# Attention scores in two bursts per unit, and products that wait for half of their operand

## The chip, the cores and the metric

The kernel runs on one core of one Trainium2 chip. The time is device microseconds of a whole execution, the median of several runs. The core has TensorE (matrix products, PE in the profile), VectorE (DVE), ScalarE (ACT), GpSimd (POOL) and SyncE (SP, which here only issues transfers), each with its own queue of instructions. Matrix products land in PSUM, which has eight banks here; only VectorE and ScalarE empty them in this kernel.

## The reference

Two layers, one behind the other. Attention without softmax, for 8 batches, 12 heads, 448 positions and 64 elements a head:

```python
scores = scale * np.matmul(q, k.transpose(0, 1, 3, 2))
attn = np.maximum(scores, 0.0) ** 2 / S
x = np.matmul(attn, v)                  # heads side by side: 3584 x 768
h = x @ w_in                            # 768 x 2048
g = np.maximum(h, 0.0) ** 2
out = g @ w_out                         # 2048 x 768
```

## The kernel before

**Units and rounds.** A batch is cut into three units of four heads, 24 units (`NUN`) in all. A unit's scores are made in seven rounds (`TJ`), one for every 64 keys, so the whole kernel has 168 rounds. A round is four matmuls of 64x64 weights and 448 columns (L522), which run at once on the four quarters of the array, and fills two PSUM banks. `squared` (L534) empties each bank with max(.,0) on VectorE (L538) or ScalarE (L541) into a `rel` tile, and squares that on ScalarE (L545) or GpSimd (L548) into an `at` tile, of which there are 11. When all seven rounds of a unit are squared, its AV (`av`, L568) multiplies them with v: 28 matmuls, again in quarters, into two banks, which VectorE or ScalarE copies to `xt` (L608, L610).

**Dense work.** When a batch's three AVs are done, `push_dense` (L946) queues its dense work. The first layer has 16 groups (`h_group`, L657), one for each block of 128 of the 2048 rows of g: six full-array matmuls of 448 columns (L650), then ScalarE squares the bank (L639) and VectorE masks by sign (L634) into the block of g. The second layer takes two chunks of 128 tokens together (`o_groups`, L833) and uses seven products in place of eight, as Strassen's method does: m1, m2, m6, m5, m7, m3, m4, each of eight matmuls of 384 columns (L863). They multiply a half of g (eight blocks), or a sum of halves (s1 to s4, VectorE, L842), with a part of w_out or a combination of parts; parts are gathered by copies (L783, L785) and by multiply-adds (L875), and go to memory.

**What a product waits for.** `evac_g` enters each masked block of g in `g_ops[b]`. `chunk` (L770) hands all of that list to `o_groups` as `ready`, so each product and each sum that reads g waits for all 16 blocks of its batch.

**The order of the work.** The kernel has manual scheduling. The program first lists operations (`plan.add`, `plan.pe`) with costs, dependencies, buffers and due times; then `Plan.simulate` plays the engines forward and writes down the order in which each engine gets its instructions. TensorE takes what is ready and due soonest. An operation can be glued to the one ahead of it (`glue`, L182): TensorE then takes that one next if it is ready, waits up to 0.45 us in the plan for it if it will be ready by then, and takes other work if not. The plan charges a switch between quarter mode and full mode at L50. `run` (L75) tries 16 rules, and with each up to six fits of the landing times of transfers, and keeps the plan that ends first among those whose landing times agree.

**The main loop** (L1100) goes over pairs of rounds. Each pair is entered as one burst, then a share of the queued dense work (`run_some`). The AV of unit n is glued behind the pair at index (7(n+1)-1)//2+2, four or five rounds after the unit's last round, and with `MERGE` the next pair is glued behind the AV, so that burst has four rounds and an AV. The first 21 rounds, the start-up and the first batch's first layer are written out before the loop.

Of the kernel before, what the change touches and what calls it, by code (L numbers as in the profile page):

```python
# [42 lines left out]
class Plan:  # L43
# [31 lines left out]
    def run(self):  # L75

        for z, op in enumerate(self.ops):
            op.id = z
        for op in reversed(self.ops):
            if not op.fixed or op.alts[0][0] != "PE":  # L80
                took = min(a[2] for a in op.alts)
                if len(op.alts[0]) > 4 and op.alts[0][4]:
                    took = 7.0
                due = min([x.due for x in op.nexts] or [1e6]) - took - 0.1
                op.due = due if op.due is None else min(op.due, due)
        start = {name: list(slots) for name, slots in self.pools.items()}, dict(self.busy)
        uses = [(b, b.left) for b in {b for op in self.ops for b in op.bufs}]

        def once(landing, rules):
            self.landing, (self.patience, self.lead) = dict(landing), rules  # L90
            self.pools = {name: list(slots) for name, slots in start[0].items()}
            self.busy, self.sent, self.order = dict(start[1]), [], []
            for b, left in uses:
                b.left, b.end, b.tile = left, 0.0, None
            self.simulate()
            return max(op.end for op in self.ops)

        best = None
        for rules in ((p, q) for p in self.PATIENCE for q in self.LEAD):
            landing: dict = {}  # L100
            for _ in range(6):
                try:
                    end = once(landing, rules)
                except RuntimeError:
                    break
                self.land()
                late = max(t - landing.get(z, 0.0) for z, t in self.landing.items())
                if late < 0.4 and (best is None or end < best[0]):
                    best = end, landing, rules
                landing = self.landing  # L110
        once(*best[1:])
        alone = None
        for emit, op in self.order:
            got = emit()
            if op is None:
                continue
            if len(op.way) > 5:
                alone = got
            elif alone is not None and op.engine == "POOL" and not op.size:
                self.behind(got, alone)  # L120
                alone = None
        return best[0]
# [175 lines left out]
def kernel(  # L298
# [11 lines left out]
    B, H, S, D = q.shape  # L310
# [5 lines left out]
    P = 128  # L316
    TP = 64
    TJ = S // TP
    NU = 3
    NUN = B * NU  # L320
# [303 lines left out]
    def evac_g(op, bank, b, fs, cols):  # L624
        g = gts[b]
        w = cols.stop - cols.start

        def views():
            src = bank.tile[:, 0:len(fs) * w].rearrange("p (f c) -> p f c", c=w)
            return src, g.tile[:, fs[0]:fs[-1] + 1, cols]  # L630

        def mask():
            src, dst = views()
            nc.vector.scalar_tensor_tensor(  # L634
                out=dst, in0=src, scalar=0.0, in1=dst, op0=ALU.is_gt, op1=ALU.mult)

        def sq():
            src, dst = views()
            nc.scalar.activation(out=dst, in_=src, func=AF.Square)  # L639

        one = plan.add([act(len(fs) * w, sq)], [op], [bank, g], due=plan.now + 0.3)
        two = plan.add([dve(len(fs) * w, mask)], [one], [bank, g], due=plan.now + 0.9)
        g_ops.setdefault(b, []).append(two)

    def h_mms(bank, b, f, cols, c0):
        w = cols.stop - cols.start
# [40 lines left out]
    def h_first():  # L687

        work = []
        for two in range(2):  # L690
# [28 lines left out]
            def turn(two=two, buf=buf, marks=marks):  # L719
# [8 lines left out]
                def copy(fn):  # L728
# [2 lines left out]
                        ps.tile.bitcast(FP16).rearrange("p (f c) -> p f c", c=P))  # L731

                op = plan.pe(0.057 * NH, flip, list(marks), [ps, buf])
                g_ops.setdefault(0, []).append(plan.add(
                    [("DVE", 0.62, 0.7, copy(nc.vector.tensor_copy)),
                     ("ACT", 0.93, 1.02, copy(nc.scalar.copy))], [op], [ps, g],
                    due=plan.now + 0.3))

            work += [(0.2157 * NM, wide(z, 2 * two + z)) for z in range(2)]
            work.append((0.057 * NH, turn))  # L740
# [14 lines left out]
    LO, HI = slice(0, HALF), slice(HALF, DM)  # L755
    rests: dict = {}

    def rest(pr):
        buf = Buf("rest")
        ops = []  # L760
        for i in range(2):
            b = 2 * pr + i

            def emit(i=i, b=b):
                return nc.gpsimd.tensor_copy(buf.tile[:, :, 64 * i:64 * i + 64],  # L765
                                             gts[b].tile[:, :, 3 * P:S])
            ops.append(plan.add([("POOL", 1.55, 1.6, emit)], g_ops[b], [buf, gts[b]]))
        rests[pr] = ops, buf

    def chunk(b, c):  # L770
        return (lambda: g_ops[b], lambda: gts[b], lambda: gts[b].tile[:, :, c * P:(c + 1) * P],
                [(b, 2 * c), (b, 2 * c + 1)])

    def rest_chunk(pr):
        return (lambda: rests[pr][0], lambda: rests[pr][1], lambda: rests[pr][1].tile,
                [(2 * pr, TJ - 1), (2 * pr + 1, TJ - 1)])

    def copied(op, bank, part):
# [54 lines left out]
    def o_groups(one, two):  # L833
# [11 lines left out]
        def sums():  # L845
            vec = nc.vector
            combine("s1", vec.tensor_add, ready2(), [buf2()],
                    lambda: view2()[:, lo], lambda: view2()[:, hi])
            combine("s2", vec.tensor_sub, ready1() + [st["s1"][0]], [buf1(), st["s1"][1]],
                    lambda: st["s1"][1].tile, lambda: view1()[:, lo])  # L850
            combine("s3", vec.tensor_sub, ready1() + ready2(), [buf1(), buf2()],
                    lambda: view1()[:, lo], lambda: view2()[:, lo])
            combine("s4", vec.tensor_sub, ready1() + [st["s2"][0]], [buf1(), st["s2"][1]],
                    lambda: view1()[:, hi], lambda: st["s2"][1].tile)

        def product(bank, lhs, deps, srcs, w, first, last=True):
# [28 lines left out]

        def m1():
            sums()
            op = product("x", lambda: view1()[:, lo], ready1() + [w2_ops[0][0]], [buf1()],
                         w2[0][0], True)
            part("r1", "x", op)  # L890

        def m2():
            op = product("y", lambda: view1()[:, hi], ready1() + [w2_ops[0][1]], [buf1()],
                         w2[0][1], True)
            close(at1, LO, "y", op, "r1")

# [19 lines left out]
            close(at1, HI, "z", op, "r2")  # L916

        def m4():
            op = product("w", lambda: view2()[:, hi], ready2() + t_ops["t4"], [buf2()], t4, True)
            close(at2, LO, "w", op, "r3", -1.0)  # L920

        return [(0.1625 * NH, fn) for fn in (m1, m2, m6, m5, m7, m3, m4)]
# [64 lines left out]
    EARLY = 6  # L987
    PLAIN0 = False
    NPE = 6
    MERGE = True  # L990
    ROUNDS = NUN * TJ
    NB = ROUNDS // 2
    STREAM = NU * TJ

    def av_burst(n):
        return (TJ * (n + 1) - 1) // 2 + 2

    pushes = {av_burst(NU * b + 2): b for b in range(1, B)}
    avs = {av_burst(n): n for n in range(NU, NUN)}

    idle = pools["part"][0].bitcast(FP16)[:, 0:512]
    nc.vector.memset(idle, 0.0)
# [91 lines left out]
    push_dense(0)  # L1094

    def coming(n):
        return plan.now + 4.5 * (TJ * n - 2 * i) / 2

    skipped, chain = 0, None
    for i in range(STREAM // 2, NB):  # L1100
        rs = [divmod(r, TJ) for r in range(max(STREAM, 2 * i), 2 * i + 2)]
        for n in range(NU, NUN):
            if i == max(STREAM // 2, TJ * (n - 2) // 2 + 1):
                if n >= EARLY:
                    for w in "kq":
                        raws[n, w] = load_qk(n, w, max(50.0, coming(n) - 20.0), n < EARLY + 2)
                if n not in vst:
                    load_v(n, coming(n) - 6.0)
            if i == max(STREAM // 2, (TJ * (n - 1) + 1) // 2 - 2) and n > 3:
                if n >= EARLY:  # L1110
                    for w in "kq":
                        casts[n, w] = cast_qk(n, w, raws[n, w])
# [3 lines left out]
                else:  # L1116
                    for w in "kq":
                        turn_dma(n, w, casts[n, w])
        todo = []
        for n, t in rs:  # L1120
            sp = [Buf("mm"), Buf("mm")]
            op = scores([(n, t)], sp, WHOLE, False)
            todo.append((op, sp, n, t))
            if chain is not None:
                chain.glue = op
            chain = op
        for op, sp, n, t in todo:
            second, at = square(op, sp, S)
            ats[n, t] = second, at, lambda tl: tl
        if i in avs:  # L1130
            last, chain = chain, av(avs[i], list(range(TJ)))
            last.glue = chain
        if i in pushes:
            push_dense(pushes[i])
        if i in avs and MERGE and i + 1 < NB:
            skipped = 1
            continue
        nxt = min([j for j in pushes if j > i] or [NB + 2])
        run_some(max(0.0, (queued - 4.0) * (1 + skipped) / (nxt - i + skipped)))
        skipped, chain = 0, None  # L1140
    run_some(3.0)
    for j in sorted(j for j in avs if j >= NB):
        av(avs[j], list(range(TJ)))
    for j in sorted(j for j in pushes if j >= NB):
        push_dense(pushes[j])
    ending = True
    run_some(1e9)
    plan.run()
# [30 lines left out]
```

## Time and profile before

The median of three runs is 381.44 us (380.92 to 383.48); the profiled execution spans 380.1 us.

| | busy us | share of the span | instructions |
|---|---|---|---|
| TensorE matmuls | 369.7 | 97% | 3277 |
| VectorE | 274.9 | 72% | 468 |
| ScalarE | 272.8 | 72% | 592 |
| GpSimd | 220.7 | 58% | 270 |

Busy time of TensorE counts from an instruction's start to its modelled end, and successive matmuls overlap; so rates are better read from the starts of rows than from their durations. In a row of the timeline the columns are start and duration in us, engine, line, operation, result and operands, shape and count; a bracket at the end is idle time of the engine ahead of the row and what ended it. The chain of work that ended last is followed back from the last instruction, at each step to what released it or to the instruction before it on its engine.

### The profile page before, as it was taken

How to read it: one execution, taken by the hardware profiler on the slowest of the kernel's cores; microseconds unless marked ns; L12 is line 12 of the kernel's file. 1: busy time of each engine (PE TensorE's matmuls, PEld its weight loads, DVE VectorE, ACT ScalarE, POOL GpSimd, SP SyncE). 2: the span in 40 equal slices, each digit the busy share in tenths (PEclk: the TensorE clock that was granted, in tenths of full speed). 3: DMA queues.
4: the chain of work that ended last, by engine and by line, in shares of the span. 5: the costliest groups of instructions: out<-in, count | busy, mean ns of one | idle time of the engine just before them, and what ended most of it. 6: DMA issues, size and time to landing. Idle time of an engine off the chain costs nothing.

```text
span 380.1 us, 8791 instructions
## 1 busy us (share of the span) xinstructions
PE 369.7 (97%) x3277; PEld 195.5 (51%) x3277; DVE 274.9 (72%) x468; ACT 272.8 (72%) x592; POOL 220.7 (58%) x270
## 2 busy tenths in 40 slices
PE   7899999999999999999999999999999999999995
PEld 3545655444455445444554555545555545555563
DVE  2996899977987787577997576676796668256731
ACT  4998999787956897697887675886795785244221
POOL 7999886596877786486663856574781343000100
PEclk9999999999999999999999999999999999999999
DMA  9999998699759943878347864685443002210243
GB/s 182 185 207 203 204 230 239 143 200 136 180 154 214 221 113 75 174 211 134 81 111 184 209 164 75 187 173 137 88 94 95 3 0 60 62 26 0 64 104 83
DMA packets 70218, 51.36 MB, mean 135 GB/s; under 512 B 36896, under 2 KB 70176, under 8 KB 70176
## 3 DMA queue, kind: packets, MB, share of 16 engines
q1 hardware_dynamic: 52384, 35.86, 38.8%
q0 software_dynamic: 16928, 14.09, 25.3%
q10 hardware_dynamic: 864, 0.85, 0.7%
q8 instruction: 25, 0.41, 0.4%
q14 instruction: 17, 0.14, 0.1%
HBM read 45.61 MB, written 11.01 MB: 149 GB/s over the span
## 4 chain that ended last, share of the span: by engine, by line
PE 89%; POOL 3%; DVE 3%; DMA 2%; ACT 1%; issue 1%; POOLq 0%; DVEq 0%
PE mm L650 38%; PE mm L863 32%; PE mm L522 9%; PE mm L588 8%; DMA g<-in_k_dram 2%; DVE comb L842 1%; DVE rel L538 1%; POOL w L496 1%; POOL comb L548 1%; PE mm L460 1%; PE mm L699 1%; POOL vs L489 1%; ACT at L545 1%; POOL g L406 0%; ACT g L729 0%
## 5 line engine op out<-in xcount | busy, mean ns | idle before, releaser
L548 POOL TENSOR_TENSOR at<-rel 128x448 f16<-128x448 f32 (+1 forms) x147 | 132.8, 924 | 62.7 <-DVE rel L538 43.9
L650 PE MATMUL mm<-xt,w 128*128 128x448 f16 (+1 forms) x768 | 148.7, 346 | 0.0
L634 DVE SCALAR_TENSOR_TENSOR g<-mm,g 128x448 f16<-128x448 f32 (+1 forms) x128 | 77.2, 605 | 45.3 <-ACT g L639 45.1
L538 DVE TENSOR_SCALAR rel<-mm 128x448 f32<-128x448 f32 (+3 forms) x174 | 96.8, 595 | 18.0 <-PE mm L522 16.8
L650 PEld LDWEIGHTS <-w 128*128 128x128 f16 x768 | 72.2, 98 | 71.1 <-issue 12.4
L639 ACT ACTIVATE g<-mm 128x448 f16<-128x448 f32 (+1 forms) x128 | 68.9, 540 | 46.3 <-PE mm L650 44.8
L545 ACT ACTIVATE at<-rel 128x448 f16<-128x448 f32 (+1 forms) x189 | 100.3, 586 | 0.8 <-PE mm L588 0.5
L541 ACT ACTIVATE rel<-mm 128x448 f32<-128x448 f32 (+2 forms) x174 | 84.6, 547 | 6.1 <-PE mm L522 5.8
L863 PEld LDWEIGHTS <-comb 128*128 128x128 f16 x448 | 42.4, 98 | 33.9 <-issue 5.2
L440 POOL CAST blk<-raw 128x896 f16<-128x896 f32 x36 | 33.9, 953 | 33.0 <-issue 7.7
L522 PE MATMUL mm<-qkt,qkt 64*64 64x448 f16 (+2 forms) x756 | 51.3, 337 | 0.8 <-DVE rel L538 0.4
L783 ACT ACTIVATE part<-mm 128x384 f32<-128x384 f32 x46 | 22.7, 500 | 39.7 <-PE mm L863 39.6
L875 DVE SCALAR_TENSOR_TENSOR part<-mm,part 128x384 f32<-128x384 f32 x56 | 30.4, 552 | 18.9 <-ACT part L783 11.5
L863 PE MATMUL mm<-wt,comb 128*128 128x384 f16 x224 | 39.5, 326 | 0.6 <-DVE comb L842 0.6
L863 PE MATMUL mm<-w,comb 128*128 128x384 f16 x224 | 39.6, 327 | 0.3 <-DVE part L785 0.3
L863 PEld LDWEIGHTS <-g 128*128 128x128 f16 x288 | 27.6, 98 | 20.7 <-issue 2.8
L588 PE MATMUL mm<-at,vs 64*64 64x448 f16 (+1 forms) x672 | 35.2, 343 | 0.2
L863 PE MATMUL mm<-w,g 128*128 128x384 f16 x192 | 33.7, 326 | 0.0
L489 POOL DMA_DIRECT2D vs<-in_v_dram x48 | 30.0, 632 | 2.6 <-DMA g<-in_k_dram 1.9
L522 PEld LDWEIGHTS <-qkt 64*64 64x64 f16 x756 | 17.7, 105 | 25.3 <-issue 21.1
L588 PEld LDWEIGHTS <-vs 64*64 64x64 f16 x756 | 21.8, 107 | 14.3 <-issue 3.2
L765 POOL COPY rest<-g 128x1024 f16<-128x1024 f16 x8 | 8.8, 1096 | 32.7 <-DVE comb L842 32.4
(59 smaller groups left out, 201.5 us busy)
## 6 DMA issues: line engine op xcount, KB each, us to landing
out_dram<-part SPq DMA_DIRECT2D x108, 96.0 KB, 2.2
raw<-in_k_dram SPq DMA_DIRECT2D x18, 448.0 KB, 4.0
raw<-in_q_dram SPq DMA_DIRECT2D x18, 448.0 KB, 4.8
vs<-in_v_dram POOLq DMA_DIRECT2D x48, 112.0 KB, 4.6
w<-in_moe_w_in_dram POOLq DMA_DIRECT2D x4, 768.0 KB, 12.0
w<-in_moe_w_out_dram POOLq DMA_DIRECT2D x4, 768.0 KB, 13.5
g<-in_k_dram POOLq DMA_DIRECT2D x4, 224.0 KB, 11.2
g<-in_q_dram POOLq DMA_DIRECT2D x4, 224.0 KB, 10.3
```

Source lines behind the costliest of these rows:

```text
L440: return lambda: fn(blk.tile.rearrange("p t (f d) -> p f t d", f=2), tile_of().rearrange("p f (t d) -> p f t d", d=D))
L489: return lambda: nc.gpsimd.dma_start(out=buf.tile[64 * r:64 * r + 64], in_=src[:, u, hs])
L522: nc.tensor.matmul(sp[e].tile[64 * c:64 * c + 64, c0:c0 + w].rearrange("p (t c) -> p t c", c=TP), lhsT=kT[r, t, 64 * e:64 * e + 64], rhs=q ...
L538: dve(width, lambda: nc.vector.tensor_scalar(out=r.tile[:, 0:width], in0=bank.tile[:, 0:width], scalar1=0.0, scalar2=SK, op0=ALU.max, op1= ...
L541: act(width, lambda: nc.scalar.activation(out=r.tile[:, 0:width], in_=bank.tile[:, 0:width], func=AF.Relu, scale=SK))],
L545: act(width, lambda: nc.scalar.activation(out=dst(), in_=r.tile[:, 0:width], func=AF.Square)),
L548: lambda: nc.gpsimd.tensor_mul(dst(), r.tile[:, 0:width], r.tile[:, 0:width]))],
L588: nc.tensor.matmul(banks[f].tile[64 * e:64 * e + 64, c0:c0 + w], lhsT=vs[r, e ^ c, t * D:(t + 1) * D], rhs=a[r, e, :], start=(t == 0), sto ...
L634: nc.vector.scalar_tensor_tensor(out=dst, in0=src, scalar=0.0, in1=dst, op0=ALU.is_gt, op1=ALU.mult)
L639: nc.scalar.activation(out=dst, in_=src, func=AF.Square)
L650: nc.tensor.matmul(bank.tile[:, c0:c0 + w], lhsT=w1[f // 4][:, m, f % 4 * P:(f % 4 + 1) * P], rhs=xts[b].tile[:, m, cols], start=(m == 0), ...
L863: nc.tensor.matmul(buf.tile[:, 0:HALF], lhsT=lhs()[:, j, :], rhs=w[:, j, :], start=(first and j == 0), stop=(j == NH - 1), skip_group_chec ...
```

## The change

Four things change.

1. The loop over pairs gives way to a list of bursts. Up to round 41 it repeats the old bursts. From unit 6 on (the third batch) each unit has two: four rounds, with the AV of the unit before glued in between the second and the third, and then three rounds. The dense work is shared out by rounds. The aim is fewer changes between small matmuls and dense ones.
2. `g_ops` keeps for each block which half of g and which columns it fills, and `filled` picks those that a reader needs: the products and sums that read one half of g wait for that half alone.
3. The plan tries up to ten fits of the landing times for each rule, and from the fifth on a landing time only moves later.
4. Loads and transposes of q and k are entered when the first round of a burst has reached their mark.

The diff, cut to its core:

```diff
-            for _ in range(6):
+            for turn in range(10):
...
+                if turn > 3:
+                    for z, t in self.landing.items():
+                        self.landing[z] = max(t, landing.get(z, 0.0))
...
-        g_ops.setdefault(b, []).append(two)
+        g_ops.setdefault(b, []).append((two, fs[0] // NH, cols))
...
+    def filled(b, half, cols):
+        return [op for op, h, c in g_ops[b]
+                if half in (None, h) and c.start < cols.stop and cols.start < c.stop]
...
-            combine("s2", vec.tensor_sub, ready1() + [st["s1"][0]], [buf1(), st["s1"][1]],
+            combine("s2", vec.tensor_sub, ready1(0) + [st["s1"][0]], [buf1(), st["s1"][1]],
...
-            combine("s3", vec.tensor_sub, ready1() + ready2(), [buf1(), buf2()],
+            combine("s3", vec.tensor_sub, ready1(0) + ready2(0), [buf1(), buf2()],
...
-            combine("s4", vec.tensor_sub, ready1() + [st["s2"][0]], [buf1(), st["s2"][1]],
+            combine("s4", vec.tensor_sub, ready1(1) + [st["s2"][0]], [buf1(), st["s2"][1]],
...
-            op = product("x", lambda: view1()[:, lo], ready1() + [w2_ops[0][0]], [buf1()],
+            op = product("x", lambda: view1()[:, lo], ready1(0) + [w2_ops[0][0]], [buf1()],
...
-            op = product("y", lambda: view1()[:, hi], ready1() + [w2_ops[0][1]], [buf1()],
+            op = product("y", lambda: view1()[:, hi], ready1(1) + [w2_ops[0][1]], [buf1()],
...
-            op = product("w", lambda: view2()[:, hi], ready2() + t_ops["t4"], [buf2()], t4, True)
+            op = product("w", lambda: view2()[:, hi], ready2(1) + t_ops["t4"], [buf2()], t4, True)
...
+    FIRST = (((21,), None), ((22, 23), None), ((24, 25), None), ((26, 27), None), ((28, 29), None),
+             (range(30, 34), 3), ((34, 35), None), ((36, 37), None), (range(38, 42), 4))
+    STEPS = (0, 1, 2, 3), (4, 5, 6)
...
+    def bursts():
+        for rs, n in FIRST:
+            yield list(rs), n
+        for n in range(2 * NU, NUN):
+            r = TJ * n
+            for step in STEPS:
+                yield [r + z for z in step], (n - 1 if step[0] == 0 else None)
+        yield [], NUN - 1
...
-    for i in range(STREAM // 2, NB):
+    for steps, done in bursts():
...
+        for z, r in enumerate(steps):
+            if z == 2 and done is not None:
+                chain = link(av(done, list(range(TJ))))
+            n, t = divmod(r, TJ)
+            sp = [Buf("mm"), Buf("mm")]
+            chain = op = link(scores([(n, t)], sp, WHOLE, False))
+            second, at = square(op, sp, S)
...
+            run_some(max(0.0, (queued - 4.0) * len(steps) / (nxt + 3 - now)))
```

More of the change, by code (lines that the diff above doesn't have):

```diff
@@ L733, in turn @@
                 op = plan.pe(0.057 * NH, flip, list(marks), [ps, buf])
-                g_ops.setdefault(0, []).append(plan.add(
+                done = plan.add(
                     [("DVE", 0.62, 0.7, copy(nc.vector.tensor_copy)),
                      ("ACT", 0.93, 1.02, copy(nc.scalar.copy))], [op], [ps, g],
-                    due=plan.now + 0.3))
+                    due=plan.now + 0.3)
+                g_ops.setdefault(0, []).append((done, two, PARTS[0]))
             work += [(0.2157 * NM, wide(z, 2 * two + z)) for z in range(2)]
@@ L766, in emit @@
                                              gts[b].tile[:, :, 3 * P:S])
-            ops.append(plan.add([("POOL", 1.55, 1.6, emit)], g_ops[b], [buf, gts[b]]))
+            ops.append(plan.add([("POOL", 1.55, 1.6, emit)], filled(b, None, slice(3 * P, S)), [buf, gts[b]]))
         rests[pr] = ops, buf
     def chunk(b, c):
-        return (lambda: g_ops[b], lambda: gts[b], lambda: gts[b].tile[:, :, c * P:(c + 1) * P],
+        cols = slice(c * P, (c + 1) * P)
+        return (lambda half=None: filled(b, half, cols), lambda: gts[b], lambda: gts[b].tile[:, :, cols],
                 [(b, 2 * c), (b, 2 * c + 1)])
     def rest_chunk(pr):
-        return (lambda: rests[pr][0], lambda: rests[pr][1], lambda: rests[pr][1].tile,
+        return (lambda half=None: rests[pr][0], lambda: rests[pr][1], lambda: rests[pr][1].tile,
                 [(2 * pr, TJ - 1), (2 * pr + 1, TJ - 1)])
@@ L989 @@
     NPE = 6
-    MERGE = True
+    FIRST = (((21,), None), ((22, 23), None), ((24, 25), None), ((26, 27), None), ((28, 29), None),
+             (range(30, 34), 3), ((34, 35), None), ((36, 37), None), (range(38, 42), 4))
+    STEPS = (0, 1, 2, 3), (4, 5, 6)
     ROUNDS = NUN * TJ
-    NB = ROUNDS // 2
     STREAM = NU * TJ
[L995 to L999, printed above, removed]
+    def bursts():
[6 more added lines that the diff above has]
+        yield [], NUN - 1
     idle = pools["part"][0].bitcast(FP16)[:, 0:512]
@@ L1096, in coming, with reached @@
     def coming(n):
-        return plan.now + 4.5 * (TJ * n - 2 * i) / 2
-    skipped, chain = 0, None
-    for i in range(STREAM // 2, NB):
-        rs = [divmod(r, TJ) for r in range(max(STREAM, 2 * i), 2 * i + 2)]
+        return plan.now + 2.25 * (TJ * n - now)
+    seen: set = set()
+    def reached(what, n, at):
+        if now < at or (what, n) in seen:
+            return False
+        seen.add((what, n))
+        return True
+    for steps, done in bursts():
+        now = steps[0] if steps else ROUNDS
         for n in range(NU, NUN):
-            if i == max(STREAM // 2, TJ * (n - 2) // 2 + 1):
+            if reached("load", n, TJ * (n - 2) + 2):
                 if n >= EARLY:
@@ L1108 @@
                     load_v(n, coming(n) - 6.0)
-            if i == max(STREAM // 2, (TJ * (n - 1) + 1) // 2 - 2) and n > 3:
+            if n > 3 and reached("turn", n, TJ * (n - 1) - 5):
                 if n >= EARLY:
@@ L1118, with link @@
                         turn_dma(n, w, casts[n, w])
[L1119 to L1123, printed above, removed]
+        chain, todo = None, []
+        def link(op):
             if chain is not None:
                 chain.glue = op
-            chain = op
-        for op, sp, n, t in todo:
+            return op
+        for z, r in enumerate(steps):
[4 more added lines that the diff above has]
+            chain = op = link(scores([(n, t)], sp, WHOLE, False))
             second, at = square(op, sp, S)
             ats[n, t] = second, at, lambda tl: tl
[L1130 to L1145, printed above, removed]
+        if not steps:
+            run_some(3.0)
+            av(done, list(range(TJ)))
+        if done is not None and done % NU == NU - 1:
+            push_dense(done // NU)
+        if steps:
+            nxt = min(TJ * NU * z for z in range(1, B + 1) if TJ * NU * z > now)
+            run_some(max(0.0, (queued - 4.0) * len(steps) / (nxt + 3 - now)))
     ending = True
```

## The prediction

> **What bounds the kernel now.** I read the page's totals first, then the chain of work that ended last, then the waits of TensorE, then its timeline.
>
> ```profile
> PE 369.7 (97%) x3277; PEld 195.5 (51%) x3277; DVE 274.9 (72%) x468; ACT 272.8 (72%) x592; POOL 220.7 (58%) x270
> ...
> PE 89%; POOL 3%; DVE 3%; DMA 2%; ACT 1%; issue 1%; POOLq 0%; DVEq 0%
> ```
>
> TensorE is busy for 97% of the span and carries 89% of the chain; the other engines have over a quarter of their time free. By stretches, TensorE is idle for 5.2 us of the first 50 us (4.6 us of it in the first 25, while the first inputs arrive), for 0.96 us between 100 and 150 us, not at all from 150 to 349 us, and for about 4 us after its last matmul. So the part that the change touches (from about 66 us on) is a queue of TensorE work with one small hole. Only fewer or cheaper TensorE microseconds, or that hole, can be gained there.
>
> A busy engine isn't one at its peak, so I looked for time hidden inside the busy stretches. These are TensorE's rows around the AV of one unit (start, duration, line, operation, tiles, count):
>
> ```profile
> 249.58 0.57 PE L522 MATMUL mm<-qkt,qkt 64*64 64x448 f16 x8
> 250.09 3.58 PE L650 MATMUL mm<-xt,w 128*128 128x448 f16 x18
> 253.60 0.57 PE L522 MATMUL mm<-qkt,qkt 64*64 64x448 f16 x8
> 254.00 1.49 PE L588 MATMUL mm<-at,vs 64*64 64x448 f16 x28
> 255.32 0.55 PE L522 MATMUL mm<-qkt,qkt 64*64 64x448 f16 x8
> 255.81 1.47 PE L863 MATMUL mm<-w,comb 128*128 128x384 f16 x8
> 257.12 1.46 PE L863 MATMUL mm<-wt,comb 128*128 128x384 f16 x8
> 258.42 4.70 PE L650 MATMUL mm<-xt,w 128*128 128x448 f16 x24
> 263.05 0.57 PE L522 MATMUL mm<-qkt,qkt 64*64 64x448 f16 x8
> ```
>
> Start to start gives the real rates. In the tail 96 matmuls of L650 run from 330.24 to 348.40, 0.1892 us each; the 168 of L863 after them take 27.3 us, 0.1626 each; 28 matmuls of the AV here take 1.32 us, 0.0471 each, four quarter arrays at a time. Now one cycle of "two score rounds, then dense work": 253.60 - 249.58 = 4.02 us. The work in it is 18 x 0.1892 = 3.406 and 8 x 0.0471 = 0.377. So 0.24 us are neither. The next cycle, 263.05 - 253.60 = 9.45 us, holds 44 x 0.0471 = 2.072, 16 x 0.1626 = 2.602 and 24 x 0.1892 = 4.541, and leaves 0.235 us, though it has 44 small matmuls and not 8. The loss belongs to the visit to the 64x64 mode and not to the rounds in it: **0.235 us per burst**, counted as busy.
>
> **What the skill says.** The Trainium skill, "TensorEngine Tiling (Array Packing)", Key Properties, states "Mode switching requires drain", and gives no price; the two cycles above agree and price it at 0.235 us there and back. The same page, PSUM Bottleneck, warns that tiling speeds up TensorE and not the emptying of PSUM: here a round takes 0.19 us of TensorE and two copies out of 0.55 (ScalarE) to 0.62 us (VectorE). "TensorE: Matmul & The Clock Gate", Step-by-step: what each phase is for, says that matmuls stay in program order; so a matmul that waits holds every later one. "SBUF — State Buffer", SBUF: two separate sides, says that a VectorE operation with two SBUF inputs and a GpSimd operation lock each other out. The trace agrees: the same 128x1024 combination takes 0.68 us at 354 us, where GpSimd rests, and 1.42 us at 101 us, where it squares scores.
>
> **The change, part by part.**
>
> *Bursts.* No matmul is added or taken away. Up to round 41 the list of bursts repeats the old one. From round 42 (unit 6) the old loop makes 63 pairs of rounds, of which 18 are joined to the next pair by an AV: 45 bursts. The new one makes 2 per unit for 18 units: 36. The last unit's AV stands alone in both. Nine visits fewer at 0.235 us are **-2.1 us**. In the trace I count 50 visits from the AV at 66.93 us to the lone one at 324.88, against the 46 written, since the planner parted some that were meant to be glued (at 66.93, 151.37 to 159.89 and 313.85 us). If the new plan parts none, 50 - 37 = 13 visits go, -3.1 us; if it parts eight or nine, almost nothing is left.
>
> *The four-round burst* (two rounds, AV, two rounds) is what the old joined burst already is, row by row above. It costs nothing new.
>
> *The three-round burst* is the new shape. It fills six of the eight PSUM banks in about 0.6 us, and they take six copies of about 0.58 us on two engines, 1.75 us, to empty. The waiting instruction would be the third round or the first dense matmul behind it, and with them all of TensorE's queue. One such burst is already in the trace, by an accident of the plan:
>
> ```profile
> 144.07 0.76 PE L522 MATMUL mm<-qkt,qkt 64*64 64x448 f16 x12
> 144.76 1.47 PE L863 MATMUL mm<-w,rest 128*128 128x384 f16 x8
> 146.07 2.76 PE L863 MATMUL mm<-w,g 128*128 128x384 f16 x16
> 148.67 2.76 PE L863 MATMUL mm<-wt,comb 128*128 128x384 f16 x16
> ```
>
> It takes 0.69 us start to start, 12 x 0.0471 = 0.565 and 0.125 of switch, and no dense matmul behind it waits. Bounds: 0 as here; at most 18 bursts x 0.45 us (how long the planner lets TensorE hold for a glued round) = 8.1 us. I take 0: with two banks still emptying from dense groups, six are free.
>
> *The AV comes sooner.* It needs all 14 squares of its unit. The old AV of unit n stands four or five rounds after the unit's end, behind two dense stretches; the new one two rounds after, behind one. From 84.6 us (AV of unit 6) to 313.85 (AV of unit 22) a unit takes 14.3 us; less 14 x 4 x 0.0471 = 2.6 of small matmuls and two visits, 11.2 us are dense, of which three sevenths, 4.8 us, lie behind the three-round burst. With the first two rounds the AV comes about 5.2 us after the burst. The six squares of the burst at 144.07 were done at about 149.0, 4.2 us after its end at 144.76. A margin of about one us, then, while ScalarE also serves the h groups. If it fails, the planner puts dense work in and parts the burst (0.235 us), or TensorE waits up to 0.45. I charge two partings in 18, **+0.5 us**; bounds 0 and 18 x 0.45 = 8.1.
>
> *Half of g.* m1, s2 and s3 wait for the lower eight blocks, m2, m4 and s4 for the upper eight; s1 needs both. This takes waits away and adds none. It can only pay where a product really waits for g or for a sum made from it. TensorE's waits hold 0.6 us for a combination and 0.3 for a copied part, once each, and the rows there show somewhat more:
>
> ```profile
> 102.01 1.46 PE L863 MATMUL mm<-wt,comb 128*128 128x384 f16 x8
> 104.11 1.48 PE L863 MATMUL mm<-wt,comb 128*128 128x384 f16 x8 [0.63 <-DVE comb L842]
> 105.55 1.47 PE L863 MATMUL mm<-w,comb 128*128 128x384 f16 x8
> 107.35 1.46 PE L863 MATMUL mm<-w,comb 128*128 128x384 f16 x8 [0.33 <-DVE part L785]
> ```
>
> At 1.30 us each these should start at 103.31, 104.61, 105.91; the last is 1.44 us late. But VectorE is full from 98 to 110 us there, with its combinations slowed to 1.42 us by GpSimd: it is its queue that is late and not the release of g. I take a third, **-0.5 us**; bounds 0 and -1.4. Elsewhere the two old products behind the last h group (2.6 us) hide the old wait already.
>
> *Loads and the plan.* Loads of q and k are entered two rounds later in program order with their start time still counted from the coming unit; TensorE waits for no transfer after the start, so nothing. The planner tries ten fits of the landing times in place of six, with damping. This changes which of 16 rules wins, so the order everywhere, the start included; there 0.6 us of idle time between 25 and 50 us is all that isn't the first loads. I count 0, with 1 us either way.
>
> Sum: -2.1 + 0.5 - 0.5 = -2.1 us; 381.44 becomes **379.3**.
>
> **The rivals.**
> *A. Visits saved, as summed*: 379.3 (378.2 to 380.4). For it: the three-round burst that runs free, and the equal loss of bursts of unlike length. Chance 0.57.
> *B. The saving is eaten*: partings and short waits for squares or banks at half of the 18 units, 9 x 0.235 = 2.1 us: about 381.4. For it: 4 to 5 partings in the old plan already, one of them right behind the old three-round burst. Against: the fewer squares held at once, at most nine to eleven tiles of the eleven and not eleven or twelve. Chance 0.22.
> *C. Slower*: the heavier pulses of copies meet the h groups and VectorE's combinations, and TensorE waits about 0.45 us at 16 of 36 bursts, 7.2 us against 2.1 saved: 386.5. For it: VectorE and ScalarE at 72% on average have stretches at 100%, as at 98 to 110 us, and matmuls keep their order, so a wrong guess of the plan can't be repaired. Against: no wait behind any of the old bursts of 44 matmuls. Chance 0.12.
> *D. More than summed*: no parting (-3.1), the hole at 103 us gone (-1.4) and a luckier start: 377 or a little under. Chance 0.09.
>
> **How the numbers follow.** The time is that of A. The range goes from just under D, 376.9, to 384.0, past B and into the near side of C; about 0.15 is left outside. Faster by over 1% means under 377.6, which only D reaches: 0.09. Slower by over 1% means above 385.3, most of C: 0.11. Same: 0.80.
>
> **What would show it.** Right: from 66 us on some 37 to 41 visits to the 64x64 mode, rows of 12 score matmuls without idle time behind them, the dense tail at 0.1892 and 0.1626 us a matmul as now. B: many groups of 4 or 8 scores with dense work between them, visits at 45 or more. C: idle time of TensorE behind L538, L541 or L545 that recurs by unit. The forecast is wrong if TensorE's idle time after 50 us grows above 3 us, or if the start or the tail moves by over 2 us through another choice of the planner.

## The result, and the profile after

The changed kernel takes **379.36 us** (median of six runs, 379.01 to 380.24) against 381.34: a ratio of 0.9946, 95% interval 0.992 to 0.9971. On another chip, beside the experiments, it takes 379.45 us against 380.85, ratio 0.9969 (0.9954 to 0.9984); there I had expected 1.5 to 2.5 us less than before. The gain is 2.0 us by the medians on the first chip and 1.4 on the other (2.1 and 1.2 by the ratios). The experiments ran on three chips, on which the kernel before takes 380.82 to 380.92 us.

The page's totals and the chain of work that ended last, after the change:

```profile
PE 366.3 (97%) x3277; PEld 196.5 (52%) x3277; DVE 272.6 (72%) x472; ACT 269.7 (71%) x587; POOL 221.1 (59%) x271
...
PE 90%; DMA 4%; ACT 3%; POOL 1%; issue 1%; DVE 1%; ACTq 0%; POOLq 0%
```

Nothing in the shape has changed: as many matmuls, the same 97%, and the other engines within 1% of the span. TensorE's busy time is 3.4 us shorter with the same 3277 matmuls. That is where the change of mode hides: the account below puts 1.9 us of it down to eight visits fewer. TensorE's timeline around one unit, to be laid beside the stretch from 249 to 263 us of the kernel before:

```profile
243.99 0.57 PE L525 MATMUL mm<-qkt,qkt 64*64 64x448 f16 x8
244.39 1.49 PE L591 MATMUL mm<-at,vs 64*64 64x448 f16 x28
245.72 0.55 PE L525 MATMUL mm<-qkt,qkt 64*64 64x448 f16 x8
246.20 6.98 PE L653 MATMUL mm<-xt,w 128*128 128x448 f16 x36
253.11 0.76 PE L525 MATMUL mm<-qkt,qkt 64*64 64x448 f16 x12
253.81 1.47 PE L873 MATMUL mm<-w,comb 128*128 128x384 f16 x8
255.12 1.46 PE L873 MATMUL mm<-wt,comb 128*128 128x384 f16 x8
256.42 4.70 PE L653 MATMUL mm<-xt,w 128*128 128x448 f16 x24
261.05 0.57 PE L525 MATMUL mm<-qkt,qkt 64*64 64x448 f16 x8
```

From the four-round burst at 243.99 to the next at 261.05 us the work is 56 x 0.0471 + 60 x 0.1892 + 16 x 0.1626 = 16.59 us of 17.06, so two visits to the 64x64 mode cost 0.47 us. It is the change of mode and not any change of operation that costs: from 255.12 to 256.42, where one dense operation gives way to another, eight matmuls take 1.30 us, their plain 8 x 0.1626.

**One account for all kernels.** Take TensorE's rows from about 44 us on, start to start, and subtract every matmul at the rate of the dense tail (0.1892 and 0.1626 us) or of the AV (0.0471). What remains, the loss, is switches and holes. From the start of one visit to the start of the next the loss has a median of 0.230 us where the visit holds 4 small matmuls (50 cycles of all the traces), 0.232 for 8 (252), 0.231 for 12 (153) and 0.236 for 44 (195). So I charge 0.235 a visit, as in the prediction, and call the rest holes. "Median" is each kernel's own, and the ratio is to the kernel before on the same chip. The table counts from the first matmul behind 44 us, so a visit at that edge can fall in or out.

| kernel | median us | ratio (95% interval) | visits | loss us | holes us |
|---|---|---|---|---|---|
| before | 381.34 | 1 | 56 | 14.6 | 1.4 |
| changed | 379.36 | 0.9946 (0.992 to 0.9971) | 48 | 12.1 | 0.8 |
| changed, another chip | 379.45 | 0.9969 (0.9954 to 0.9984) | 48 | 12.3 | 1.0 |
| bursts alone | 381.33 | 1.0009 (0.9993 to 1.0024) | 47 | 13.4 | 2.3 |
| half-waits alone | 381.69 | 1.0019 (1.0003 to 1.0035) | 54 | 14.3 | 1.6 |
| ten fits alone | 380.43 | 0.9996 (0.9979 to 1.0012) | 55 | 15.3 | 2.4 |
| changed, no half-waits | 381.97 | 1.0025 (1.0013 to 1.0038) | 47 | 13.8 | 2.7 |
| changed, two bursts from unit 4 | 380.03 | 0.9978 (0.9962 to 0.9994) | 46 | 12.8 | 2.0 |
| changed, four bursts a unit | 388.33 | 1.0199 (1.0162 to 1.0236) | 81 | 21.2 | 2.2 |
| changed, three rounds with the AV, then four | 384.88 | 1.0102 (1.006 to 1.0144) | 59 | 17.4 | 3.5 |
| no half-waits, two products held back | 380.93 | 0.9998 (0.998 to 1.0016) | 48 | 13.9 | 2.7 |
| changed, two products held back | 380.91 | 1.0000 (0.9987 to 1.0013) | 48 | 12.7 | 1.5 |
| before, two products held back | 382.16 | 1.0041 (1.0029 to 1.0054) | 56 | 14.8 | 1.6 |
| changed, seven PSUM banks | 388.45 | 1.0198 (1.0168 to 1.0227) | 63 | 20.1 | 5.3 |

The last three columns are of one profiled execution each. That of the kernel before (span 380.1 us) took 381.87 us, 0.5 above the median on its own chip, and its span lies 1.1 us above the median beside the experiments (379.0 us); that of the changed kernel (377.4) is near its own there (377.65); the traced execution of the ten fits alone was 1.8 us slower than their median. So the 2.7 us between the two traces overstate the gain by about one at most; the visits aren't in doubt, since they are fixed by the program, but the holes of a single trace are.

### The profile page after: what moved, and what is told of

Its sections match the earlier page's. It is cut to its first block, busy times and chain, and to the rows that moved or that the text cites. A ratio compares the mean times of both kernels' runs of the same rounds, so it can differ in the third digit from the quotient of the medians.

```text
span 377.4 us, 8786 instructions
## 1 busy us (share of the span) xinstructions
PE 366.3 (97%) x3277; PEld 196.5 (52%) x3277; DVE 272.6 (72%) x472; ACT 269.7 (71%) x587; POOL 221.1 (59%) x271
## 4 chain that ended last, share of the span: by engine, by line
PE 90%; DMA 4%; ACT 3%; POOL 1%; issue 1%; DVE 1%; ACTq 0%; POOLq 0%
PE mm L653 38%; PE mm L873 34%; PE mm L525 9%; PE mm L591 7%; DMA w<-in_moe_w_in_dram 2%; DMA g<-in_k_dram 2%; PE mm L702 1%; ACT at L548 1%; PE mm L463 1%; ACT rel L544 1%; ACT part L793 0%; POOL vs L492 0%; DVE rel L541 0%; DVE part L885 0%; POOL comb L551 0%
## 5 line engine op out<-in xcount | busy, mean ns | idle before, releaser
L551 POOL TENSOR_TENSOR at<-rel 128x448 f16<-128x448 f32 (+1 forms) x148 | 133.9, 928 | 68.1 <-DVE rel L541 50.3
L653 PEld LDWEIGHTS <-w 128*128 128x128 f16 x768 | 73.1, 98 | 67.9 <-issue 7.4
L642 ACT ACTIVATE g<-mm 128x448 f16<-128x448 f32 (+1 forms) x128 | 69.8, 546 | 49.5 <-PE mm L653 49.2
L541 DVE TENSOR_SCALAR rel<-mm 128x448 f32<-128x448 f32 (+3 forms) x172 | 94.8, 594 | 12.0 <-PE mm L525 10.8
L548 ACT ACTIVATE at<-rel 128x448 f16<-128x448 f32 (+1 forms) x188 | 98.9, 593 | 0.3 <-DVE rel L541 0.3
L525 PE MATMUL mm<-qkt,qkt 64*64 64x448 f16 (+2 forms) x756 | 49.1, 336 | 0.9 <-DVE rel L541 0.4
L885 DVE SCALAR_TENSOR_TENSOR part<-mm,part 128x384 f32<-128x384 f32 x56 | 30.5, 554 | 24.8 <-ACT part L793 13.4
L793 ACT ACTIVATE part<-mm 128x384 f32<-128x384 f32 x42 | 21.1, 505 | 35.3 <-PE mm L873 34.5
L443 POOL CAST blk<-raw 128x896 f16<-128x896 f32 x36 | 33.3, 931 | 21.2 <-DVE wt L839 6.5
L525 PEld LDWEIGHTS <-qkt 64*64 64x64 f16 x756 | 18.7, 105 | 23.9 <-issue 18.7
```

The lines of the kernel that those rows point to most:

```text
L443: return lambda: fn(blk.tile.rearrange("p t (f d) -> p f t d", f=2), tile_of().rearrange("p f (t d) -> p f t d", d=D))
L525: nc.tensor.matmul(sp[e].tile[64 * c:64 * c + 64, c0:c0 + w].rearrange("p (t c) -> p t c", c=TP), lhsT=kT[r, t, 64 * e:64 * e + 64], rhs=q ...
L541: dve(width, lambda: nc.vector.tensor_scalar(out=r.tile[:, 0:width], in0=bank.tile[:, 0:width], scalar1=0.0, scalar2=SK, op0=ALU.max, op1= ...
L548: act(width, lambda: nc.scalar.activation(out=dst(), in_=r.tile[:, 0:width], func=AF.Square)),
L551: lambda: nc.gpsimd.tensor_mul(dst(), r.tile[:, 0:width], r.tile[:, 0:width]))],
L653: nc.tensor.matmul(bank.tile[:, c0:c0 + w], lhsT=w1[f // 4][:, m, f % 4 * P:(f % 4 + 1) * P], rhs=xts[b].tile[:, m, cols], start=(m == 0), ...
```

## The experiments

### The parts by themselves

The changed places of loads and transposes (part 4) come with the new loop and weren't tested by themselves. My theory was the sum of the prediction: visits carry the gain, and half-waits add a little. The rivals: the half-waits carry it; or another draw of the plan does, whatever the visits.

*Bursts alone*: the new list of bursts, but `filled` hands out all of g, and six fits.

```diff
     def filled(b, half, cols):
         return [op for op, h, c in g_ops[b]
-                if half in (None, h) and c.start < cols.stop and cols.start < c.stop]
+                if True]
...
-            for turn in range(10):
+            for turn in range(6):
...
-                if turn > 3:
+                if turn > 9:
```

> The two bursts per unit alone: every product and sum waits for all of g as before, and the plan makes six fits. It has 51 visits to the 64x64 mode from unit 3 on, as the changed kernel has, against 59 before. If the visits carry the gain at 0.22 us each, 8 fewer give -1.8 us: 379.5, and the hole near 103 us, where TensorE waited 1.4 us for VectorE's sums, may stand or not. If the half-waits carry it, it stays at 381.

Measured: 381.33 us. The saved visits are in the trace (nine in the stretch of the table, -2.1 us), and the time doesn't fall. By the trace, holes take 0.9 us more than before: 0.6 us at 58.7 us behind the AV of unit 4, 0.7 at 79.6 in and behind a burst of four rounds, 0.5 at 88.6 and 0.4 at 255.8 behind three-round bursts. That would leave -1.2 us. The medians don't show it, and the trace of the kernel before, which is 0.5 to 1.1 us slow, may hold more holes than its usual execution.

*Half-waits alone*: the changed file with the old loop over pairs, and six fits.

> The half-waits alone: the pairs of rounds and the six fits as before. It has 57 visits, two fewer than before: -0.4 us. If the half-waits close the hole near 103 us, another -1.1 to -1.4: 379.6 to 379.8. If they do nothing, as VectorE's queue is late there and not the release of g: 380.9.

Measured: 381.69 us. The place near 103 us is free of holes, as one branch had it, but holes of 0.2 to 0.8 us appear between 61 and 75 us, where the first batch's products run. Neither branch said so.

*Changed, without half-waits*: the first edit above, with ten fits.

> The changed kernel with every product and sum waiting for all of g again; bursts and ten fits stay. 51 visits. If the half-waits are idle: 379.4 as the changed kernel. If they are worth the hole: 380.5 to 380.8, and the hole is back in the trace behind a VectorE sum.

Measured: 381.97 us, 2.5 us above the changed kernel (379.45, on another chip; the kernel before differs by 0.1 us between the two) and worse than either branch. TensorE's rows where batch 1 ends:

```profile
98.79 0.76 PE L525 MATMUL mm<-qkt,qkt 64*64 64x448 f16 x12
99.89 1.16 PE L525 MATMUL mm<-qkt,qkt 64*64 64x448 f16 x8 [0.34 <-DVE rel L541]
100.98 1.47 PE L873 MATMUL mm<-wt,g 128*128 128x384 f16 x8
102.38 0.38 PE L525 MATMUL mm<-qkt,qkt 64*64 64x448 f16 x4
103.39 2.76 PE L873 MATMUL mm<-wt,comb 128*128 128x384 f16 x16 [0.63 <-ACT rel L544]
```

And the same place in the changed kernel, with VectorE's row that masks the last block of g:

```profile
98.34 0.76 PE L525 MATMUL mm<-qkt,qkt 64*64 64x448 f16 x12
99.43 1.46 PE L873 MATMUL mm<-w,g 128*128 128x384 f16 x8 [0.34 <-DVE rel L541]
100.73 1.46 PE L873 MATMUL mm<-wt,g 128*128 128x384 f16 x8
102.12 0.57 PE L525 MATMUL mm<-qkt,qkt 64*64 64x448 f16 x8
```

```profile
99.83 0.62 DVE L637 SCALAR_TENSOR_TENSOR g<-mm,g 128x448 f16<-128x448 f32 x1
```

In the changed kernel the m1 that reads the lower half of batch 1's g (the w,g row at 99.43) is already running when VectorE begins to mask the last block of g at 99.83. Without half-waits the plan has no dense work ready there, puts five rounds in a row on TensorE (12 + 8 matmuls at 98.79 and 99.89), fills the banks, and waits three times for VectorE and ScalarE to empty them: 1.8 us against 0.4.

*Ten fits alone*: the old kernel with the new search.

> The kernel before with only the plan's ten fits. 59 visits as before, with another order on every engine. If the time follows visits and holes, 381.3 within 0.5. If a new draw of the plan is worth about 2 us by itself, 379 to 383 whatever the visits.

Measured: 380.43 us: below the first branch's 380.8, and by the ratio no different from before. In the changed kernel six fits lead to the very same instructions in the same order on every engine as ten, so this part of the change does nothing in it. Without half-waits they do differ: bursts alone (six fits) take 381.33 us, the changed kernel without half-waits (ten) 381.97.

### What a visit costs

*Four bursts a unit.*

```diff
-    STEPS = (0, 1, 2, 3), (4, 5, 6)
+    STEPS = (0, 1), (2, 3), (4, 5), (6,)
...
+        if steps and len(steps) == 2 and done is not None:
+            chain = link(av(done, list(range(TJ))))
```

> The changed kernel with four bursts for each unit (2, AV; 2; 2; 1 rounds) in place of two. The written order has 84 visits against 51. At 0.22 us a visit: +7.3 us, about 386.5. If the visits cost less than the two cycles of the trace said, because TensorE's weight loads overlap the change of mode: +2 to 4 us. If small bursts save holes behind VectorE: less than +7.3 by up to 1 us.

Measured: 388.33 us, 8.9 above the changed kernel beside it, for 33 more visits: 7.8 us at 0.235 and 1.2 to 1.4 of holes more, most of them before 125 us. The price holds and the branch that had overlap is out. Three cycles of it:

```profile
228.27 1.46 PE L873 MATMUL mm<-wt,comb 128*128 128x384 f16 x8
229.66 0.57 PE L525 MATMUL mm<-qkt,qkt 64*64 64x448 f16 x8
230.16 2.44 PE L653 MATMUL mm<-xt,w 128*128 128x448 f16 x12
232.45 1.46 PE L873 MATMUL mm<-wt,comb 128*128 128x384 f16 x8
233.84 0.38 PE L525 MATMUL mm<-qkt,qkt 64*64 64x448 f16 x4
234.16 1.31 PE L653 MATMUL mm<-xt,w 128*128 128x448 f16 x6
235.39 0.57 PE L525 MATMUL mm<-qkt,qkt 64*64 64x448 f16 x8
```

A burst of four matmuls, 0.19 us of work, holds TensorE for 0.32 us, and the dense row ahead of it runs 0.09 us over its eight matmuls (233.84 - 232.45 - 1.30): 0.22 together. From start to start, 229.66 to 233.84 loses 0.23 us around eight matmuls, and 233.84 to 235.39 loses 0.23 around four.

### The banks

*Three rounds with the AV, then four.*

```diff
-    STEPS = (0, 1, 2, 3), (4, 5, 6)
+    STEPS = (0, 1, 2), (3, 4, 5, 6)
```

> The changed kernel with three rounds around the AV and then four rounds without one, which fill all eight PSUM banks. The planner parts 12 more bursts: 63 visits against 51, +2.6 us: 382.0. If banks are the limit, TensorE also shows idle time behind the copies out of PSUM (L541, L544) by unit, and it is 383 to 386. If banks don't matter, 382.0 and no such idle time.

Measured: 384.88 us, 5.4 above the changed kernel: 11 more visits in the stretch of the table are 2.6 us, and the holes 2.5 to 2.7 more. The time is that of the branch where banks are the limit, but the holes don't recur by unit: the planner left four of the four-round bursts whole and parted the others.

*Seven banks.*

```diff
-        "mm": fixed(psum, "mm", 8, [P, 512], FP32),
+        "mm": fixed(psum, "mm", 7, [P, 512], FP32),
...
-        nc.tensor.matmul(pools["mm"][7], lhsT=idle[:, 0:P], rhs=idle, start=True, stop=True)
+        nc.tensor.matmul(pools["mm"][6], lhsT=idle[:, 0:P], rhs=idle, start=True, stop=True)
```

> The changed kernel with seven PSUM banks in place of eight. Three-round bursts fill six. The planner parts many: 66 visits against 51, +3.3 us, 382.8. If the idle time behind three-round bursts (0.4 us each time it appears) is the wait for a bank, such holes also recur at most of its ten remaining three-round bursts, +2 to 4 us more: 385 to 387. If they are something else, they stay as few as now.

Measured: 388.45 us, 9.0 above the changed kernel. The 15 more visits are as expected (3.5 us at 0.235). The holes take 4.3 to 4.4 us more, above the expected 2 to 4, and at 43.8 us TensorE has 1.5 to 2.3 us more work still to do, which I hadn't expected. The hole recurs behind seven of the ten three-round bursts, about 0.4 us each:

```profile
129.59 0.76 PE L525 MATMUL mm<-qkt,qkt 64*64 64x448 f16 x12
130.69 4.70 PE L653 MATMUL mm<-xt,w 128*128 128x448 f16 x24 [0.34 <-DVE rel L541]
...
142.54 0.76 PE L525 MATMUL mm<-qkt,qkt 64*64 64x448 f16 x12
143.64 2.62 PE L653 MATMUL mm<-xt,w 128*128 128x448 f16 x13 [0.34 <-DVE rel L541]
```

With eight banks 253.81 follows 253.11 without a hole; with seven the dense row starts 1.10 us after the burst and not 0.70. So in this kernel three rounds are about what eight banks carry; I read it as six banks of scores and two for dense work. In the changed kernel the same 0.4 us shows once behind its 16 whole three-round bursts, at 98.34.

### Is it ready work that was missing?

Batch 0 uses up all its products before batch 1's h groups, so none is left to stand behind them. I held two back.

```diff
-    QUOTA = (7, 14, 9, 12, 12, 13, 12, 99)
+    QUOTA = (5, 14, 9, 12, 12, 13, 12, 99)
```

> The changed kernel without half-waits (381.97 us), but two of the seven products of batch 0 are held back until behind the h groups of batch 1 (the quota of batch 0 is 5 in place of 7). If the half-waits pay because no other dense work is ready near 100 us, where batch 1's last blocks of g are still being masked, these two products take their place: the holes there (1.8 us together) go and it is 379.5 to 380.5. If half-waits pay by shorter waits elsewhere, it stays at 382.

Measured: 380.93 us, 1.0 less than without the held products (by the medians of two sets), and no hole from 72 to 250 us:

```profile
97.73 2.76 PE L873 MATMUL mm<-w,g 128*128 128x384 f16 x16
100.43 0.76 PE L525 MATMUL mm<-qkt,qkt 64*64 64x448 f16 x12
101.12 2.77 PE L873 MATMUL mm<-wt,comb 128*128 128x384 f16 x16
```

It wasn't enough for the expected 380.5, since holes open where the products were taken from: 1.1 us at 62.7 behind a VectorE sum, and 1.2 in all within and behind a burst from 69.8 to 71.5. For the kernel with the new bursts and no half-waits, then, what was missing near 100 us is ready work.

> The kernel before with the same two products held back. 60 visits against 59. If its hole of 1.4 us between 102 and 107 us is lack of ready dense work: 379.7 to 380.2. If it is VectorE's queue with its combinations at 1.42 us, they come in the same place and it stays near 380.9.

Measured: 382.16 us. The place near 103 us is free of holes here too, but those between 62 and 77 us cost 1.2 us by the trace. Both branches miss the time. Nor does the run tell them apart: VectorE makes the sum that TensorE had waited for (`comb<-comb,g`) at 100.12 here, ahead of another (`comb<-g,g`) at 101.77, and most of its sums take 0.68 to 0.8 us and not 1.42. What the kernel before waits for is read from its own trace, below. The run is still of use beside the one above: with two products held back, the new bursts without half-waits take 1.2 us less than the old loop (380.93 and 382.16 us on one chip).

> The changed kernel with the same two products held back. 52 visits against 51. Its hole near 100 us is only 0.4 us, so the half-waits already do this work: 379.2 to 379.8. If the place near 100 us still costs it more than the rows show: 378.5 or less.

Measured: 380.91 us, against 379.45: worse than either branch, and no better than the same kernel without half-waits (380.93). Holes of 0.3 to 0.5 us stand at 52 and 58 us.

### Going further

*Two bursts per unit from unit 4 on.*

```diff
-             (range(30, 34), 3), ((34, 35), None), ((36, 37), None), (range(38, 42), 4))
+             (range(28, 32), 3), (range(32, 35), None), (range(35, 39), 4), (range(39, 42), None))
```

(and the pair 28, 29 ahead of it taken out.)

> The changed kernel with the two bursts per unit from unit 4 on in place of unit 6. 49 visits against 51: -0.4 us, 379.0. If the stretch from 50 to 100 us, where VectorE is at nine tenths, can't take the larger pulses, holes of 1 us or more open there: 380 to 381.

Measured: 380.03 us, no gain over 379.45. Two visits less, but holes of about 0.4 us behind the bursts at 87.7 and 98.2; the second branch had the time, with holes of 1 us or more. No version beat the changed kernel.

## Why the prediction was right

**The total** was 379.3 and is 379.36. That it came so close is luck in part: its terms were less good than their sum, and by the medians the gain is 2.0 us on one chip and 1.4 on another.

**Visits.** Forecast: 9 fewer at 0.235 us, less two partings, -1.6 us. Found: by the count from 65 us on, 43 against 50, -1.6 us; from 44 us on 8 fewer, -1.9. The plan parts six bursts where the old one parted four, so two more, as I had charged. I expected 37 to 41 visits as the sign of being right, and there are 43: most of the parted ones are in the first batches, where the planner parted the AVs at 65.3 and 82.2 us from the rounds ahead of them. The experiment with four bursts a unit and the equal loss of visits of 4 to 44 matmuls show the price, and that it goes with the change of mode.

**The three-round burst** at no cost: nearly so, one hole of 0.4 us in 16. But the reason I gave, six of eight banks free, is a narrow one: with seven banks about 0.4 us come back at seven of ten.

**The four-round burst and the earlier AV** cost little: TensorE's waits after 50 us name no square of scores (L548, L551). But two of the bursts hold TensorE for 0.1 to 0.3 us in the rounds behind the AV (187.71 and 217.46), with no wait named; that term I had put at nothing.

**Half of g.** Forecast -0.5 us; in the traces the hole of 1.4 us becomes one of 0.4, -1.0, and the 0.4 stands behind a burst, where I read a wait for a bank. By these traces the term was half of what it should have been. In a usual execution it may be less: the two traces that show a large hole at this place, of the kernel before and of the ten fits alone (1.8 us), are of executions 0.5 to 1.1 and 1.8 us above their medians, and no trace of a usual one was kept. I read right that VectorE's queue was late in the kernel before "and not the release of g", but missed what the half-waits do to that queue. These are VectorE's masks and sums before, one row of TensorE, and two of VectorE's sums after:

```profile
98.08 0.61 DVE L634 SCALAR_TENSOR_TENSOR g<-mm,g 128x448 f16<-128x448 f32 x1
101.29 1.42 DVE L842 TENSOR_TENSOR comb<-g,g 128x1024 f16<-128x1024 f16 x1
102.63 1.42 DVE L842 TENSOR_TENSOR comb<-comb,g 128x1024 f16<-128x1024 f16 x1
109.24 1.47 PE L863 MATMUL mm<-w,g 128*128 128x384 f16 x8
```

```profile
87.55 0.69 DVE L852 TENSOR_TENSOR comb<-g,g 128x1024 f16<-128x1024 f16 x1
88.16 0.68 DVE L852 TENSOR_TENSOR comb<-g 128x1024 f16<-128x1024 f16 x1
```

Before, the last mask of batch 1 is done at 98.69. TensorE waits until 104.11 for the sum that ends at 104.05 (s2), while a product whose g is complete stands behind it in TensorE's order, at 109.24. That sum had waited in VectorE's queue behind s3 (`comb<-g,g`), which needs the lower halves alone. After, the s3 of batch 1's two pairs of chunks are made at 87.55 and 88.16, while the upper blocks are still being masked.

**The sum itself** was the larger error of reasoning. I added the parts, as if each brought its own share. Bursts alone give 1.0009 and half-waits alone 1.0019: together they give 0.9946 to 0.9969. Each plan has holes of its own. With ten fits and no half-waits TensorE lacks a product near 100 us, which the half-waits supply. With six fits the bursts alone have theirs in and behind bursts at 58.7, 79.6, 88.6 and 255.8 us. Half-waits alone have them at 61 to 75 us; why the plan orders that place so is a matter of its search, and I haven't isolated it. Rival B, "the saving is eaten", is thus the truth for the bursts by themselves, and the chance of 0.22 for it was the right kind of doubt.

That the gain needs both parts is shown for these plans alone. With two products held back the new bursts gain 1.2 us without half-waits, and half-waits add nothing to them; and holding back costs the kernel before 1.3 us and the changed one 1.5. A new draw of the plan can be worth as much as the gain.

**The plan.** I gave the ten fits 1 us either way. They change nothing in the changed kernel, and alone nothing measurable.

**The start**, which I counted at 0: TensorE's work still to do at 43.8 us differs by 0.1 us between the two traces. In the second trace of the changed kernel, the same program, it is 0.8 us less.

## What to carry to other kernels

Where an engine is 97% busy, look for time inside its busy rows: start-to-start times less the steady rate price a change of mode that no wait shows. Before making bursts longer, count the banks that they fill and the ready work that will stand behind them; a saving of a fraction of a microsecond per burst is lost with the first hole. And test two edits that serve one plan apart, together, and on a second plan: here neither paid alone on the first, and one did on the second.

## What the hardware showed

A visit of TensorE to the 64x64 mode and back costs 0.23 to 0.24 us, whether it holds 4, 8, 12 or 44 matmuls. About 0.1 us of it lies ahead of the visit and 0.13 behind its start (at 253.11 in the changed kernel: the 36 dense matmuls ahead take 6.91 us for 6.81, the 12 small ones 0.70 for 0.57). It shows as busy time. A change of operation within the 128x128 mode costs nothing that these traces show.
